# Attention and dense layer for one decoded token: early projection and half of a value unit moved into the loop, bias rows on four partitions, last value chunks of 48, 8, 8 tiles

## The chip, the cores and the metric

One core of one Trainium2 chip. Times are device microseconds (us) of an execution; a kernel is executed several times and the medians and single times are quoted. The kernel before takes 669.57 us (median of three, 669.31 to 669.69).

## The reference, cut to what matters

```python
# B=8 batch rows, one token each, D=512; 32 query heads, 8 key/value heads, 8192 cached positions, Dh=128
mod = (silu(c) @ w_mod).reshape(8, 6, 1, -1)            # six modulation vectors
h = layernorm(x) * (1 + ca) + sa
q = (h @ wq).reshape(B, 1, 32, 128)
p = softmax(q @ k_cache^T * Dh ** -0.5)                 # per batch row: 16 MiB of keys
o = p @ v_cache                                         # per batch row: 16 MiB of values
x = x + ga * (o.reshape(B, 1, 4096) @ wo)               # output projection, wo is 4 MiB
h = layernorm(x) * (1 + cb) + sb
x = x + gb * (relu(h @ w1 + b1) ** 2 @ w2 + b2)         # two dense layers, F = 1792
```

All tensors are bf16. The caches are 268 of the 284 MB that the kernel moves.

## The kernel before

Keys and values stream through a ring of four 4 MiB slots. One pass of a hardware loop works on one batch row: four key units, softmax, four value units 0 to 3. The program is recorded as a list of operations, each with its dependences; a helper then gives every engine its instruction stream, with a loop of eight passes. The output of eight heads is projected once, behind the loop (the part called "post").

The part that turned out to matter is how the helper writes the loop:

```python
def _looped(self, e, eng, passes):
    ...
    for i in range(passes):
        for p in "ab":
            for j, o in enumerate(self._part(e, (i, p))):
                want = self._want(e, o, i)
                # semaphores that are counted per pass: the wait stays with its instruction
                inside = {s: v for s, v in want.items() if s in per}
                ...
                # all others: the wait is written here, ahead of the loop
                self._emit(eng, None, {s: v for s, v in want.items() if s not in per}, seen)
    with nc.Fori(0, passes, engines=[pe], ...) as i:
        for j, o in enumerate(self._part(e, (0, "a"))):
            self._emit(eng, o, first["a", j], seen)
        ...
        with eng.If(i < passes - 1):          # part "b": not in the last pass
            for j, o in enumerate(self._part(e, (0, "b"))): ...
    for o in self._part(e, "post"):           # the tail
        self._emit(eng, o, self._want(e, o, passes - 1), after)
```

A slot of the ring is loaded again as soon as TensorE releases it, four units ahead. So each load is issued when TensorE reaches a certain place in its work. The loads at the start, in the order of the queue:

```python
load(0)
load(1)                                              # two key units of pass 1
d_b1 = dma("sync", s_bb, ... b1_row <- B_b1)
d_b2 = dma("sync", s_bb, ... b2_row <- B_b2)
d_wo = dma("sync", s_wo, ... wo_sb <- A_wo)          # 4 MiB, output projection
load(2)
load(3)
...
def project(k_oP):                                   # called once, in "post"
    for g in range(6):
        for j in range(4):
            t = op("tensor", ... e.matmul(bank(7)[32 * j:32 * (j + 1), :], oP[:, g, ...],
                    wo_sb[:, 4 * g + j, :], start=(g == 0), stop=(g == 5), ...), [k_oP, d_wo])
```

The last value unit (unit 3 of pass 8) arrives in four pieces that end at tiles 64, 96, 112 and 128 of 128, and TensorE takes them up one by one; behind them come the weights of the two dense layers.

Of the kernel before, what the change touches and what calls it, by code (L numbers as in the profile page):

```python
# [5 lines left out]
ACT = mybir.ActivationFunctionType  # L6
ALU = mybir.AluOpType
# [161 lines left out]
def bass_adaLN_cond__gqa_block_cached__dense_activation_squared_relu__decode_kernel(  # L169
# [17 lines left out]
    with ExitStack() as es:  # L187
# [29 lines left out]
        ONE8 = sb("ONE8", [1, B], BF16)  # L217
        PERM = sb("PERM", [128, 4, 32], BF16)
# [8 lines left out]
        b_row = sb("b_row", [1, F + D], BF16)  # L227
# [26 lines left out]
        oP = KF[:, 2816:3072].rearrange("p (g j b) -> p g j b", g=8, j=4)  # L254
        proj = KF[:, 4096:5120].bitcast(FP32)
        b1_row, b2_row = b_row[:, 0:F], b_row[:, F:F + D]
# [23 lines left out]
        s_last = [sem(f"d_l{i}") for i in range(4)]  # L280
# [25 lines left out]
        t = pool(lambda e: e.memset(ONE8[:], 1.0))  # L306
# [33 lines left out]
        t = select(PERM[:], [[-1, 4], [-4, 32]], 0, 1, 1.0, NE, t)  # L340
# [7 lines left out]
        CH = (64, 96, 112, 128)  # L348
        F2 = FT - 2

        def load(n):
            kv, b, p = units[n]
            s = n % NSLOT
            src = (A_k_cache if kv == "k" else A_v_cache)[b, 2 * p:2 * p + 2]
            src = src.rearrange("g s d -> (g s d)").rearrange("(p f) -> p f", p=128)
            dep = [released.get(s)]
            if units[n] == last:
                t0, toks = 0, []
                for i, t1 in enumerate(CH):
                    toks.append(dma("sync", s_last[i], lambda e, a=t0 * DH, z=t1 * DH: e.dma_start(  # L360
                        RING[:, s, a:z], src[:, a:z]), dep))
                    t0 = t1
                loaded[n] = toks
            else:
                loaded[n] = dma("sync", s_ring[s], lambda e: e.dma_start(slot(s), src), dep)
# [75 lines left out]

        k_sb = op("vector", lambda e: e.tensor_copy(hbT[:, :, 1, :], mod(3)), [k_modT])
# [6 lines left out]
        d_b1 = dma("sync", s_bb, lambda e: e.dma_start(b1_row, B_b1.rearrange("(o f) -> o f", o=1)))  # L449
        d_b2 = dma("sync", s_bb, lambda e: e.dma_start(b2_row, B_b2.rearrange("(o f) -> o f", o=1)))  # L450
# [56 lines left out]
        hT_ps = [bank(i)[:, 0:16 * 7].rearrange("p (f a b) -> p f a b", f=7, a=2) for i in range(2)]  # L507
        yT_ps = bank(2)[:, 0:KT * B].rearrange("p (k b) -> p k b", k=KT)

        def permute(q0, q1, dst, deps):  # L510
            pP = bank(6)[:, 64 * q0:64 * q1].rearrange("p (g j b) -> p g j b", j=4, b=B)
            for hl in range(REP):
                for j in range(4):
                    t = op("tensor", lambda e, hl=hl, j=j: e.matmul(
                        pP[32 * hl:32 * (hl + 1), :, j, :].rearrange("p (q h) b -> p h q b", h=2),
                        PERM[:, j, :], oTn_p[:, :, q0:q1, hl, :], start=True, stop=True,
                        tile_position=(0, 32 * hl)), deps)
            return op("vector", lambda e: e.tensor_copy(dst, pP), [t])

        def project(k_oP):  # L520
            for g in range(6):
                for j in range(4):
                    t = op("tensor", lambda e, g=g, j=j: e.matmul(
                        bank(7)[32 * j:32 * (j + 1), :], oP[:, g, :, :].rearrange("p j b -> p (j b)"),
                        wo_sb[:, 4 * g + j, :], start=(g == 0), stop=(g == 5), tile_position=(0, 32 * j)),
                        [k_oP, d_wo])
            return op("vector", lambda e: e.tensor_copy(proj, bank(7)), [t])

        for b in range(B):
# [23 lines left out]
            pe_stream(1, 4)  # L553
# [5 lines left out]
            pe_stream(1, 4)  # L559
# [32 lines left out]
            turn_acts(pe_stream(3, 1))  # L592
# [3 lines left out]
            pe_stream(2, 1)  # L596
# [9 lines left out]
            for p in range(NP):  # L606
                if p == NP - 1:
                    Pg.at = "post" if lastb else (b, "b")
# [3 lines left out]
                lastu = units[n] == last  # L612
                if not lastu:
                    for m in range(32):
                        cg = m % 4
                        t = op("tensor", lambda e, p=p, m=m, cg=cg, vt=vt, Obank=Obank: e.matmul(  # L616
                            Obank[32 * cg:32 * (cg + 1), :], lhs[:, p, 32 * m:32 * m + 32],
                            vt[:, 4 * m:4 * m + 4, :], start=(m < 4), stop=(m >= 28),
                            tile_position=(0, 32 * cg)),
                            [loaded[n], k_rinv] + pmd[m // 8])  # L620
# [3 lines left out]
                    elif p == NP - 2:  # L624
                        pe_stream(3, 4)
# [13 lines left out]
                    elif p == NP - 2:  # L639
                        pe_stream(1, 4)  # L640
# [3 lines left out]
                    if lastb and p == NP - 2:  # L644
                        Pg.at = "post"
                        k_proj = project(permute(0, 3, oP[:, 0:6], [norm_last, k_all] + stg_free + hold))
                        for k in range(KT):
                            op("tensor", lambda e, k=k: e.matmul(
                                yT_ps[:, k, :], b2_row[:, k * 128:(k + 1) * 128], ONE8[:, :],
                                start=(k == 0), stop=False, skip_group_check=True), [d_b2, s_bank_free[2]])  # L650
                else:
# [15 lines left out]
                    def direct(a, z, i):  # L667
                        for m in range(a, z):
                            t = op("tensor", lambda e, m=m: e.matmul(
                                oT_w, vt[:, m, :], wide(lhs[:, NP - 1, 8 * m:8 * m + 8]), start=False,  # L670
                                stop=(m == z - 1), skip_group_check=True), [loaded[n][i], k_rinv] + pmd[m // 32])
                        return t

                    for m in range(28):
                        cg = m % 4
                        t = op("tensor", lambda e, m=m, cg=cg, vt=vt: e.matmul(
                            bank(3)[32 * cg:32 * (cg + 1), :], lhs[:, NP - 1, 32 * m:32 * m + 32],
                            vt[:, 4 * m:4 * m + 4, :], start=(m < 4), stop=(m >= 24),
                            tile_position=(0, 32 * cg)),
                            [loaded[n][0 if m < 16 else 1 if m < 24 else 2], k_rinv] + pmd[m // 8])  # L680
                        if m == 15:
                            for f in range(FT):
                                op("tensor", lambda e, f=f: e.matmul(
                                    hT_ps[f // 7][:, f % 7, 1, :], fcol(b1_row, f), ONE8[:, :],
                                    start=(f % 7 == 0), stop=False, skip_group_check=True), [d_b2, s_bank_free[f // 7]])
                            for k in range(KT):
                                op("tensor", lambda e, k=k: e.matmul(
                                    attn_ps[:, k, :], proj[:, 128 * k:128 * (k + 1)], SELP[:, :],
                                    start=(k == 0), stop=False, skip_group_check=True), [k_proj])
                    osb = O_sb[:, 1, :]  # L690
                    t = op("vector", lambda e: e.tensor_copy(osb, bank(3)), [t])
                    for i in range(4):
                        op("tensor", lambda e, i=i: e.matmul(
                            oT_ps, osb[:, i * 128:(i + 1) * 128], SEL[:, i, :], start=(i == 0), stop=False,
                            skip_group_check=True), [t, k_all])
                    t = direct(112, 128, 3)
# [3 lines left out]
                    k_oP = permute(3, 4, oP[:, 6:8], [t])  # L700
                    for g in (6, 7):
                        for j in range(4):
                            for k in range(KT):
                                k_attn = op("tensor", lambda e, g=g, j=j, k=k: e.matmul(
                                    attn_ps[:, k, :], wo_sb[:, 4 * g + j, k * 128:(k + 1) * 128], oP[:, g, j, :],
# [9 lines left out]
        o_ps = bank(4)[:, 0:256]  # L715
        for cc in range(2):
            for k in range(2):
                op("tensor", lambda e, k=k, cc=cc: e.matmul(
                    o_ps[64 * cc:64 * cc + B, 128 * k:128 * (k + 1)], x1T[:, 2 * cc + k, :], IDENT[:, :],
                    start=(k == 0), stop=False, tile_position=(0, 64 * cc), skip_group_check=True), [k_x1])  # L720
# [9 lines left out]
        rsb = rstd2[:].unsqueeze(1).to_broadcast([128, 7, B])  # L730
        for k in range(KT):
# [4 lines left out]
            for f in range(FT):  # L736
                t = op("tensor", lambda e, f=f, k=k: e.matmul(
                    hT_ps[f // 7][:, f % 7, :, :], wcol(k, f), hbT[:, k, :, :], start=False, stop=(k == KT - 1),
                    skip_group_check=True), [k_hb, k_sb, d_w1[k // (KT - 1)]])
                if k == KT - 1 and f % 7 == 6:  # L740
                    hh = f // 7
                    fs = slice(7 * hh, 7 * (hh + 1))
                    t = op("vector", lambda e, hh=hh, fs=fs: e.tensor_tensor(
                        rT[:, fs, :], hT_ps[hh][:, :, 0, :], rsb, ALU.mult), [t, k_rstd])
# [3 lines left out]
                        hidT[:, fs, :], rT[:, fs, :], 0.0, rT[:, fs, :], ALU.max, ALU.mult), [t]))  # L748
        for f in range(FT):
            for k in range(KT):  # L750
                t = op("tensor", lambda e, f=f, k=k: e.matmul(
                    yT_ps[:, k, :], W2v[:, f, k * 128:(k + 1) * 128], hidT[:, f, :],
                    start=False, stop=(f == FT - 1), skip_group_check=True), [k_sq[f // 7], d_w2[f // 4]])
# [47 lines left out]
```

## Time and profile before

| | before |
|---|---|
| median (range) | 669.57 us (669.31 to 669.69) |
| span of the profiled execution | 667.6 us |
| TensorE busy | 513.8 us, 77% |
| a pass of the loop | 77.6 to 77.7 us, DMA share 1.00 |
| last weights landed | 664.16 us |

### The profile page before, as it was taken

To read this page: it belongs to the slowest core of one execution; us is meant where nothing else is said; L and a number is where in the kernel's file an instruction comes from. 1 tells how busy PE (TensorE), PEld (TensorE's weight loads), DVE (VectorE), ACT (ScalarE), POOL (GpSimd) and SP (SyncE) were. 2 spreads that over 40 slices of the span, in tenths; PEclk is the share of its full clock that TensorE was granted. 3 is DMA by queue.
4 is the path that set the end of the run, shared out by engine and by line. 5 is a ranking of instruction groups with operands and counts; after the bars stand their busy time and mean duration, and the time that the engine had idled before them with its cause. 6 is when DMAs were issued, how large, how long until landed. Compare 5 with 4: busy or idle time off the path is not lost.

```text
span 667.6 us, 15485 instructions
## 1 busy us (share of the span) xinstructions
PE 513.8 (77%) x7064; PEld 344.8 (52%) x7064; DVE 302.6 (45%) x571; ACT 258.7 (39%) x289; POOL 18.4 (3%) x76
## 2 busy tenths in 40 slices
PE   3493984898739985699848987499756998389885
PEld 2283731675328742577317853287425773177534
DVE  2262731566216651367314662166513673156722
ACT  2151640466105660266404662066502654046610
POOL 7300000000000000000000000000000000000000
PEclk9696997899969998699977999699987999779996
DMA  9999999999999999999999999999999999999996
GB/s 376 431 412 437 426 427 435 432 430 430 434 434 430 430 432 436 428 432 432 436 428 430 434 434 430 430 434 434 428 432 434 434 426 434 432 434 428 434 415 264
DMA packets 12176, 283.85 MB, mean 425 GB/s; under 512 B 1250, under 2 KB 1283, under 8 KB 3588
## 3 DMA queue, kind: packets, MB, share of 16 engines
q1 hardware_dynamic: 12116, 283.65, 99.1%
q8 instruction: 9, 0.15, 0.1%
q10 hardware_dynamic: 48, 0.02, 0.0%
q14 instruction: 3, 0.02, 0.0%
HBM read 283.66 MB, written 0.01 MB: 425 GB/s over the span
## 4 chain that ended last, share of the span: by engine, by line
PE 52%; DMA 37%; ACT 7%; DVE 2%; SPq 1%; issue 1%
PE PS L479 36%; DMA ring<-in_A_k_cache_dram 32%; PE PS L496 9%; ACT P_sb L562 5%; PE PS L616 2%; DMA ring<-in_B_w_dram 2%; DMA ring<-in_A_wq_dram 2%; PE PS L469 1%; SPq L659 1%; ACT KTb L484 1%; DVE O_sb L626 1%; PE PS L463 1%; PE PS L574 1%; DVE Pm L588 0%; PE PS L594 0%
## 5 line engine op out<-in xcount | busy, mean ns | idle before, releaser
L484 ACT ACTIVATE KTb<-PS 128x1024 bf16<-128x1024 bf16 x192 | 196.5, 1024 | 332.2 <-PE PS L479 332.2
L479 PE MATMUL PS<-IDENT,ring 128*128 128x128 bf16 x4096 | 267.4, 227 | 51.2 <-DMA ring<-in_A_k_cache_dram 51.2
L479 PEld LDWEIGHTS PS<-IDENT,ring 128*128 128x128 bf16 x4096 | 246.8, 102 | 99.6 <-DMA ring<-in_A_k_cache_dram 52.4
L486 DVE COPY KTb<-PS 128x1024 bf16<-128x1024 bf16 x320 | 210.1, 687 | 143.9 <-PE PS L479 141.8
L616 PE MATMUL PS<-ring,Pm 128*32 128x512 bf16 x992 | 70.4, 434 | 46.8 <-DMA ring<-in_A_v_cache_dram 45.9
L496 PE MATMUL PS<-KTb,Qb 128*32 128x512 bf16 x1024 | 78.8, 385 | 4.5 <-ACT KTb L484 4.5
L626 DVE CAST O_sb<-PS 128x512 bf16<-128x512 f32 x31 | 21.4, 692 | 126.7 <-PE PS L616 126.7
L616 PEld LDWEIGHTS PS<-ring,Pm 128*32 128x32 bf16 x992 | 26.8, 106 | 85.5 <-DMA ring<-in_A_v_cache_dram 54.4
L562 ACT ACTIVATE P_sb<-PS,negm 128x1024 bf16<-128x1024 f32 x32 | 35.2, 1112 | 20.2 <-DVE negm L557 20.2
L469 PE MATMUL PS<-ONES 128*128 128x512 f32 x80 | 42.1, 630 | 0.0
L574 PE MATMUL PS<-IDENT,P_sb 128*128 128x128 bf16 x256 | 19.9, 220 | 15.4 <-ACT P_sb L562 15.4
L588 DVE COPY Pm<-PS 64x512 bf16<-64x512 bf16 x48 | 20.2, 421 | 25.0 <-PE PS L574 24.5
L574 PEld LDWEIGHTS PS<-IDENT,P_sb 128*128 128x128 bf16 x256 | 14.4, 98 | 25.1 <-ACT P_sb L562 25.1
L463 PE MATMUL PS<-IDENT 128*128 128x512 bf16 x88 | 26.9, 380 | 0.0
L496 PEld LDWEIGHTS PS<-KTb,Qb 128*32 128x32 bf16 x1024 | 15.4, 94 | 21.1 <-ACT KTb L484 8.5
L503 DVE TENSOR_REDUCE m<-PS 128x1 f32<-128x512 f32 x32 | 22.0, 689 | 6.6 <-PE PS L496 6.6
L630 PEld LDWEIGHTS PS<-SEL,O_sb 128*128 128x128 bf16 x124 | 5.8, 97 | 30.5 <-DVE O_sb L626 30.5
L469 PEld LDWEIGHTS PS<-ONES 128*128 128x128 f32 x80 | 12.7, 190 | 10.6 <-issue 10.6
L630 PE MATMUL PS<-SEL,O_sb 128*128 128x8 bf16 x124 | 7.9, 169 | 12.4 <-DVE O_sb L626 12.0
L641 DVE TENSOR_TENSOR oTn<-PS,rinv 128x8 f32 x31 | 6.0, 194 | 14.9 <-PE PS L630 14.9
L463 PEld LDWEIGHTS PS<-IDENT 128*128 128x128 bf16 x88 | 7.7, 105 | 9.1 <-issue 7.2
L484 ACT ACT_TABLE_LOAD x8 | 10.3, 1283 | 3.2 <-issue 3.2
(132 smaller groups left out, 115.9 us busy)
## 6 DMA issues: line engine op xcount, KB each, us to landing
ring<-in_A_k_cache_dram SPq DMA_DIRECT2D x32, 4096.0 KB, 34.2
ring<-in_A_v_cache_dram SPq DMA_DIRECT2D x31, 4096.0 KB, 27.8
ring<-in_A_wq_dram SPq DMA_DIRECT2D x1, 4096.0 KB, 19.9
wo_sb<-in_A_wo_dram SPq DMA_DIRECT2D x1, 4096.0 KB, 47.6
ring<-in_w_mod_dram SPq DMA_DIRECT2D x1, 3072.0 KB, 10.3
ring<-in_A_v_cache_dram SPq DMA_DIRECT2D x1, 2048.0 KB, 22.6
ring<-in_B_w_dram SPq DMA_DIRECT2D x3, 512.0 KB, 19.4
ring<-in_B_w_dram SPq DMA_DIRECT2D x1, 1344.0 KB, 17.9
```

Source lines behind the costliest of these rows:

```text
L463: ts = [op("tensor", lambda e: e.matmul(bank(at).rearrange("p (a r) -> p a r", a=4), IDENT[:, :], rhs)) for _ in range(n)]
L469: ts = [op("tensor", lambda e: e.matmul(bank(at).rearrange("p (a r) -> p a r", a=4), ONES[:, :], rhs)) for _ in range(n)]
L479: t = op("tensor", lambda e, j=j, i=i: e.matmul(STG[j][:, i, :], src[:, 32 * k + 8 * j + i, :], IDENT[:, :], is_transpose=True), [loaded[n ...
L484: stg_free[j] = op("scalar", lambda e, j=j, dst=dst: e.activation(dst, STG[j], ACT.Copy), [t])
L486: stg_free[j] = op("vector", lambda e, j=j, dst=dst: e.tensor_copy(dst, STG[j]), [t])
L496: t = op("tensor", lambda e, hf=hf, q=q, rhs=rhs: e.matmul(PS[32 * q:32 * (q + 1), k, :], Qb[:, 2 * p + hf, :], rhs, start=(p == 0 and hf ...
L503: return op("vector", lambda e: e.tensor_reduce(m4[:, k:k + 1], bank(k), AX.X, ALU.max), [t])
L562: exps.append(op("scalar", lambda e, k=k: e.activation(P_sb[:, k, :, :, :], bank(k).rearrange("p (i x) -> p i x", i=8).unsqueeze(2).to_bro ...
L574: t = op("tensor", lambda e, k=k, i=i: e.matmul(STG[k][:, i, :], P_sb[:, k, i, :, :].rearrange("p h x -> p (h x)"), IDENT[:, :], is_transp ...
L588: done.append(op("vector", lambda e, dst=dst, frm=frm: e.tensor_copy(dst, frm), [t, k_pm]))
L616: t = op("tensor", lambda e, p=p, m=m, cg=cg, vt=vt, Obank=Obank: e.matmul(Obank[32 * cg:32 * (cg + 1), :], lhs[:, p, 32 * m:32 * m + 32], ...
L626: t = op("vector", lambda e, osb=osb, Obank=Obank: e.tensor_copy(osb, Obank), [t])
```

## The change

Intent: shorten what stands between the last bytes and the end. The projection of the first three value units goes ahead of unit 3, and with it the first half of unit 3, into the part of the loop that every pass executes, so that the tail starts later in the work. The biases lie on four partitions, so that 18 small matmuls become 11. The last value unit is cut so that only 8 + 8 tiles remain for the end, and four identity matmuls move between the weights of the last layer. Core of the diff (index changes, new memsets and the rearranged bias loads are cut):

```diff
-        CH = (64, 96, 112, 128)
+        CH = (64, 112, 120, 128)
...
+        def permute_early(deps):              # 4 matmuls, 1 filler, 4 copies (2 VectorE, 2 ScalarE)
...
         def project(k_oP):
             for g in range(6):
                 for j in range(4):
...
-                        [k_oP, d_wo])
-            return op("vector", lambda e: e.tensor_copy(proj, bank(7)), [t])
+                        k_oP + [d_wo])
+            return t
...
             for p in range(NP):
-                if p == NP - 1:
-                    Pg.at = "post" if lastb else (b, "b")
...
+                if p == NP - 1:
+                    proj_done = project(permute_early([norm_last, k_all] + stg_free + hold))
+                    values(0, 16, 28)
+                    Pg.at = "post" if lastb else (b, "b")
                 if not lastu:
-                    for m in range(32): ...
+                    t = values(0 if p < NP - 1 else 16, 32, 28)
...
-                    if lastb and p == NP - 2:
-                        Pg.at = "post"
-                        k_proj = project(permute(0, 3, oP[:, 0:6], ...))
-                        for k in range(KT):                       # 4 bias matmuls
...
-                    for m in range(28): ...                       # 14 bias matmuls after m == 15
+                    k_proj = op("vector", lambda e: e.tensor_copy(proj, bank(7)), [proj_done])
+                    ...                                           # 11 bias matmuls
+                    partial(range(0, 4))
+                    t = values(16, 28, 24)
...
-                    t = direct(112, 128, 3)
+                    direct(CH[1], CH[2], 2)
...
+                    t = direct(CH[2], CH[3], 3)
...                                            # five filler matmuls per pass taken out
-        o_ps = bank(4)[:, 0:256]               # 4 identity matmuls, before the first dense layer
+            if f == 8: ...                     # now inside the second dense layer
```

## The prediction

> **What bounds the kernel now.** I read the page first (engine shares, DMA line), then the windows of single passes, then the chain of waits and the timeline of the last 30 us, then the DMA view of that stretch.
>
> The program is eight passes of a loop (one batch row each: four key units, softmax, four value units 0 to 3, each unit 4 MiB) and then a tail: end of the last value unit, output projection, layer norm, two small dense layers. Page and windows of three passes of the loop:
>
> ```profile
> DMA packets 12176, 283.85 MB, mean 425 GB/s; under 512 B 1250, under 2 KB 1283, under 8 KB 3588
> 175.10:252.80 77.70, 61.23 (x841) 40.93 (x840) 36.09 (x67) 31.53 (x35) 0.00 (x0) 0.91 1.00 431
> 252.80:330.40 77.60, 61.52 (x836) 41.35 (x840) 36.47 (x66) 31.53 (x35) 0.00 (x0) 0.89 1.00 432
> 330.40:408.10 77.70, 61.92 (x836) 41.64 (x832) 36.59 (x66) 31.52 (x35) 0.00 (x0) 0.89 1.00 432
> ```
>
> The last two numbers of a window are DMA share and GB/s. The share is 1.00 in each pass, at 431 to 432 GB/s, and TensorE is busy 61 of 77.7 us: the loop is the time of its bytes (33.55 MB / 432 GB/s = 77.7 us). Nothing done by an engine there counts, unless it frees a buffer so late that the queue runs dry.
>
> The tail, in the timeline:
>
> ```profile
> 646.42 0.69 DVE L626 CAST O_sb<-PS 128x512 bf16<-128x512 f32 x1 [3.38 <-PE PS L616]
> 648.64 1.48 PE L523 MATMUL PS<-wo_sb,KTb 128*32 128x512 bf16 x24 [0.51 <-DVE KTb L518]
> 650.23 1.05 PE L676 MATMUL PS<-ring,Pm 128*32 128x512 bf16 x16
> 651.74 1.06 PE L687 MATMUL PS<-SELP,KTb 128*128 128x8 f32 x8
> 652.73 0.83 PE L676 MATMUL PS<-ring,Pm 128*32 128x512 bf16 x12
> 653.61 0.69 DVE L691 CAST O_sb<-PS 128x512 bf16<-128x512 f32 x1 [2.75 <-PE PS L676]
> 655.07 0.19 DVE L697 TENSOR_TENSOR oTn<-PS,rinv 128x8 bf16<-128x8 f32 x1 [0.76 <-PE PS L669]
> 658.30 1.53 PE L737 MATMUL PS<-hbT,ring 128*128 128x16 bf16 x42 [0.20 <-DVE hbT L724]
> 661.68 1.02 PE L751 MATMUL PS<-KTb,ring 128*128 128x8 bf16 x32 [0.98 <-DVE KTb L747]
> 663.57 1.01 PE L751 MATMUL PS<-KTb,ring 128*128 128x8 bf16 x24 [0.87 <-DMA ring<-in_B_w_dram]
> ```
>
> The chain of waits from 634 us on ends so:
>
> ```profile
> 649.42 14.74 DMA ring<-in_B_w_dram
> 664.16 0.05 issue
> 664.21 0.39 PE PS L751 x8
> 664.60 0.02 issue
> 664.62 0.20 DVE KTb L754
> ```
>
> So even here the landing of the second dense layer's weights (third piece 663.52, fourth 664.16) sets the end; 3.4 us of fixed work follow to 667.6. The compute path comes second: its first 32 matmuls of that layer end at 662.70, 0.87 us before the third piece lets it go on. What is worth gaining is thus about 0.9 to 1.5 us, and only if the landing moves.
>
> Why do the last bytes land so late? In two windows, DMA share and rate are again the last two numbers; then the DMA view of 651 to 664 us:
>
> ```profile
> 660.00:662.00 2.00, 1.02 (x28) 0.93 (x28) 1.19 (x6) 0.27 (x1) 0.00 (x0) 0.50 0.80 308
> 662.00:664.00 2.00, 1.13 (x43) 1.04 (x39) 0.22 (x1) 0.00 (x0) 0.00 (x0) 0.50 0.12 42
> q8 instruction: 2, 0.03, 1.0%
> ```
>
> A share of 0.12 is two of 16 DMA engines: stragglers. In the packet records every engine but one is done by 662.70; the last 2 KB packets of one end at 663.74. The two packets of the instruction queue are 16 KiB each, at 652.52 (1.07 us) and 661.23 (1.10 us). Before the first, no engine leads the late group at the last value piece (all done 653.74); after it a single one is late by 0.1 us (660.89 against 660.78 at the second weight piece), after the second it is 1.0 us late. I read this as one engine that carries both instruction packets.
>
> [...]the page lists nine such packets, seven during pass 1 (31.8 to 102.9 us), none in passes 2 to 8, two in the tail; and a pass has 834 matmuls, with its weight loads 1668 instructions[...]. [...]the granted clock here is 0.50 from 656 us to the end, but 128x8 matmuls still take 32 ns each (1.02 us / 32)[...].
>
> **The change part by part.**
>
> 1. Early projection in every pass. Removed per pass: five 128x512 filler matmuls (about 0.27 us each, 0.81 us for 3), 1.35 us. Added: 4 permuting matmuls (about 0.3 us by the old 16), one filler inside it, four copies of 32x192 (two VectorE, two ScalarE, about 0.36 us each by the old 128x192 cast), 24 projection matmuls at 1.48 us. They run between value units 2 and 3, where in a pass TensorE is idle from 569.84 to 576.35 us (6.5 us) waiting for unit 3. The added 2.5 us fit, and each pass keeps its 77.7 us: 0.
>
> 2. The same in the last pass. There unit 3 follows closely. Old: norm of unit 2 at 647.76, cast done 648.59, projection over 650.12. New: two copies in sequence on VectorE instead of one, 0.36 us later, so projection over about 650.6; first 16 value matmuls to 651.6.
>
> 3. Biases: 18 small matmuls (0.25 + 0.60 us) become 11, about 0.4 us. The projection's fp32 partial sums keep 1.06 us: done at 651.6 + 0.4 + 1.0 = 653.1.
>
> 4. Pieces of 64, 48, 8, 8 tiles instead of 64, 32, 16, 16. Bytes and packets are the same (4 x 128), so the fourth still lands at 654.23, and the second now where the third did, 652.97. All 12 value matmuls begin only then, behind step 3: 653.1 + 0.85 = 653.95, 0.4 us later than the old 653.56. Cast to 654.7, selection 654.75, last 8 direct matmuls instead of 16 (0.28 instead of 0.55): norm at about 655.25 against 655.07. Net +0.2 us on the compute path.
>
> 5. Four identity matmuls (0.38 us) move from before the first dense layer, where TensorE waited for VectorE anyway, to between the first 32 and the last 24 matmuls of the second. Compute path: 662.70 + 0.2 = 662.9, plus 0.3 is 663.2 before the last 24, then 24 x 32 ns = 0.77: 663.95, against 664.60 in the old. Possible gain 0.65 us, if the weights are there.
>
> 6. Instructions after the loop fall from 283 matmuls to 220, and the loop grows from 834 to 857[...]. [...]With one fetch, the late engine ends at 660.89 + 1.27 + 0.65 = 662.81. If the second packet comes after it, the fourth piece lands near 663.2 and step 5's 0.65 us come through; if just before its last packets, the landing stays at 664.1 and the gain is zero. I call it even, with a slight lean to the gain: 0.55 x 0.65 = 0.36 us.
>
> 7. Start: more memsets, and wider selects on POOL, about 1 us before the loop; the first key unit lands at 30.7 us, POOL ended at 26.85. Hidden.
>
> Sum: 669.57 - 0.4, rounded with room for the landing's own scatter: **669.1 us**.
>
> **Rivals.** (a) The landing does not move: DMA-bound to the last packet, time 669.5. For it: the chain above is DMA, and no byte is removed. (b) Second fetch harmless and the compute path not delayed by step 4: 668.5. For it: the last fetch is at the edge. (c) The later value matmuls, or a jump out of the loop in the middle of unit 3, cost more than 0.3 us and the compute path takes over: 670 or more. Against it: the old exit was hidden in a wait of 0.46 us for VectorE. (d) Fewer fillers let the clock fall in the softmax, or loop code no longer fits: every pass would suffer, but a value unit at half clock (3.6 instead of 1.9 us) still hides under DMA, with 14.7 us of loads queued when a key load is issued (561.6 to the landing of unit 3 at 576.35).
>
> **Range and chances.** Between (b) less 0.5 and (c) plus 0.3: 668.0 to 670.3. Two per cent is 13.4 us; only an unhidden 1.7 us in every pass would give that. Faster 0.01, same 0.98, slower 0.01.
>
> **What would show it.** Passes still 77.6 to 77.7 us at share 1.00; unit 3 of a pass still ended by its DMA; last value matmuls from about 653.1; norm of unit 3 near 655.25; instruction packets near 655.8 and 662.5 to 663; last weight landing near 663.2 (gain) or 664.1 (none). I am wrong if the passes change, if instruction packets appear in passes 2 to 8, or if TensorE waits at the loop's exit.

0.55 x 0.65 us is 0.36 us, and 669.57 - 0.4 came, rounded, to the 669.1 us that stand there. The "nine such packets" are the 16 KiB packets of the page's line "q8 instruction". Rival (d) can be read with what the trace of the kernel before has: in the wait of 6.5 us in front of unit 3 of pass 7 the granted clock went from 1.00 (571 to 573 us) to 0.50 (574 to 580), and the unit's matmuls took 3.60 us, against 1.91 for those of unit 2. And the waits for the last weights there ended with the last of sixteen shares: fifteen of the fourth piece had landed by 663.14 us, the last at 664.16, and the eight matmuls behind it began at 664.21.

## More of the kernel before

The prediction shows the windows, the tail and the chain of waits. What it does not show is the start. First the waits of TensorE in the kernel before: in a line stand the waiting group, what it waited for, then us in total, times and longest wait.

```profile
PE PS L479 <- DMA ring<-in_A_k_cache_dram: 51.2, 9, 10.1
PE PS L616 <- DMA ring<-in_A_v_cache_dram: 45.9, 10, 6.5
```

And the queue engine SP's timeline of its load issues (start, and time to the end of the group's last issue):

```profile
3.68 0.40 SPq L451 DMA_DIRECT2D wo_sb<-in_A_wo_dram  x1
14.59 23.87 SPq L365 DMA_DIRECT2D ring<-in_A_k_cache_dram  x2
41.47 41.43 SPq L365 DMA_DIRECT2D ring<-in_A_v_cache_dram  x4
95.68 8.03 SPq L365 DMA_DIRECT2D ring<-in_A_k_cache_dram  x3
```

TensorE waits for keys and values, and for nothing else longer than 4.5 us at a time. The value loads of pass 1 begin at 41.47 us and the key loads of pass 2 at 95.68, while the value unit in front of them lands at 110.00: the queue has 14 us of work in hand. The output weights, issued at 3.68 us, wait in no line: they are used only behind the loop.

## The result, and the profile after

| | before | after |
|---|---|---|
| executions, us | 669.57, 669.31, 669.69, 669.28 | 668.67 (profiled), 670.67, 671.37, 670.54 |
| median | 669.44 (four executions) | 670.61 |
| ratio after / before | | 1.0013, 95% interval 0.9991 to 1.0034: same |
| span of the profiled execution | 667.6 | 666.6 |
| last weights landed in it | 664.16 | 662.98 |

A ratio here is the mean time of one kernel's executions over that of the other's of the same rounds, so it is not quite the ratio of the medians. The "same" came as predicted, the number did not: 670.61 lies 0.3 us above the predicted range and 1.5 us above the predicted time. And the profiled execution, the only one of the four with a trace, is the one that took 668.67 us.

Its passes are as predicted. Two windows of one pass each (length, then busy time of PE, PEld, DVE, ACT, POOL, then clock, DMA share, GB/s), and the page's line of the instruction queue:

```profile
174.60:252.20 77.60, 65.80 (x931) 43.54 (x931) 38.09 (x70) 32.19 (x37) 0.00 (x0) 0.93 1.00 432
252.20:329.80 77.60, 61.69 (x863) 41.55 (x862) 37.20 (x68) 32.19 (x37) 0.00 (x0) 0.93 1.00 432
q8 instruction: 9, 0.15, 0.1%
```

Share 1.00 at 432 GB/s; nine instruction packets, seven of them in pass 1. So is its tail, in the timeline:

```profile
652.82 0.83 PE L641 MATMUL PS<-ring,Pm 128*32 128x512 bf16 x12
654.95 0.19 DVE L723 TENSOR_TENSOR oTn<-PS,rinv 128x8 bf16<-128x8 f32 x1 [0.56 <-PE PS L693]
661.60 1.01 PE L778 MATMUL PS<-KTb,ring 128*128 128x8 bf16 x32 [1.00 <-DVE KTb L767]
662.54 0.38 PE L774 MATMUL PS<-IDENT,x1T 128*8 128x128 bf16 x4
662.86 0.80 PE L778 MATMUL PS<-KTb,ring 128*128 128x8 bf16 x24
```

The last 24 matmuls are no longer preceded by a wait for the weights (before: 0.87 us), and no DMA stands near the end of the chain of waits any more:

```profile
661.60 1.01 PE PS L778 x32
662.61 0.31 PE PS L774 x4
662.92 0.75 PE PS L778 x24
663.70 0.20 DVE KTb L781
```

What nobody had asked about is the start. Waits of TensorE in the changed kernel:

```profile
PE PS L488 <- DMA ring<-in_A_k_cache_dram: 33.3, 6, 6.7
PE PS L488 <- DMA wo_sb<-in_A_wo_dram: 25.5, 1, 25.5
PE PS L641 <- DMA ring<-in_A_v_cache_dram: 15.2, 7, 3.3
```

The beginning of its chain of waits, and SP's load issues:

```profile
4.13 46.77 DMA wo_sb<-in_A_wo_dram
50.90 0.70 issue
51.60 6.58 PE PS L488 x64
```

```profile
15.20 23.43 SPq L369 DMA_DIRECT2D ring<-in_A_k_cache_dram  x2
63.40 29.59 SPq L369 DMA_DIRECT2D ring<-in_A_v_cache_dram  x4
105.79 3.31 SPq L369 DMA_DIRECT2D ring<-in_A_k_cache_dram  x2
```

L488 is the transposing of keys. It does not use the output weights, and yet it waits 25.5 us for them, once: TensorE's first pass begins at 51.6 us, where the first key unit had landed at about 31. The projection now stands inside the loop; the semaphore of the output weights is not counted per pass; so the helper writes its wait ahead of the loop, ahead of everything that the loop does. With TensorE 21 us late, the value loads of pass 1 are issued at 63.40 us instead of 41.47, and the first key load of pass 2 at 105.79 instead of 95.68. The value unit in front of that key load lands at 109.88. Of the 14 us in hand, 4 are left, and since DMA engines finish their shares of a unit at different times (the sixteen shares of that value unit landed between 107.93 and 109.88 us) and an idle engine's first packet of a load comes 1.0 to 1.5 us after the issue (read in late_one's trace, below; in the kernel before, the first load was issued at 0.81 us and its first packet came at 1.84), the margin is small.

### The profile page after: what moved, and what is told of

It is laid out like the page before. It is cut to its first block, busy times and chain, and to the rows that moved or that the text cites. A ratio compares the mean times of both kernels' runs of the same rounds, so it can differ in the third digit from the quotient of the medians.

```text
span 666.6 us, 15803 instructions
## 1 busy us (share of the span) xinstructions
PE 518.3 (78%) x7201; PEld 350.3 (53%) x7201; DVE 308.0 (46%) x586; ACT 264.0 (40%) x305; POOL 20.4 (3%) x79
## 4 chain that ended last, share of the span: by engine, by line
PE 55%; DMA 32%; ACT 6%; DVE 4%; issue 1%; POOL 0%; ACTq 0%; SPq 0%; DVEq 0%; POOLq 0%
PE PS L488 38%; DMA ring<-in_A_k_cache_dram 21%; PE PS L505 10%; DMA wo_sb<-in_A_wo_dram 7%; ACT P_sb L587 5%; DMA ring<-in_A_v_cache_dram 4%; PE PS L641 3%; ACT KTb L493 1%; DVE O_sb L659 1%; DVE m L512 1%; PE PS L599 1%; PE PS L550 1%; PE PS L619 0%; DVE Pm L613 0%; PE PS L478 0%
## 5 line engine op out<-in xcount | busy, mean ns | idle before, releaser
L488 PE MATMUL PS<-IDENT,ring 128*128 128x128 bf16 x4096 | 267.8, 228 | 60.7 <-DMA ring<-in_A_k_cache_dram 33.3
L488 PEld LDWEIGHTS PS<-IDENT,ring 128*128 128x128 bf16 x4096 | 247.3, 102 | 108.9 <-issue 49.4
L641 PE MATMUL PS<-ring,Pm 128*32 128x512 bf16 x1020 | 66.9, 407 | 17.9 <-DMA ring<-in_A_v_cache_dram 15.2
L542 ACT ACTIVATE KTb<-PS 32x192 bf16<-32x192 f32 x16 | 5.2, 322 | 103.6 <-PE PS L472 103.4
L550 PE MATMUL PS<-wo_sb,KTb 128*32 128x512 bf16 x192 | 15.4, 467 | 6.8 <-ACT KTb L542 6.8
L472 PE MATMUL PS<-IDENT 128*128 128x512 bf16 x48 | 15.7, 381 | 0.0
L550 PEld LDWEIGHTS PS<-wo_sb,KTb 128*32 128x32 bf16 x192 | 5.9, 108 | 14.0 <-DVE KTb L544 9.5
```

The source lines that it names most:

```text
L488: t = op("tensor", lambda e, j=j, i=i: e.matmul(STG[j][:, i, :], src[:, 32 * k + 8 * j + i, :], IDENT[:, :], is_transpose=True), [loaded[n ...
L550: t = op("tensor", lambda e, g=g, j=j: e.matmul(bank(7)[32 * j:32 * (j + 1), :], oPe[:, 3 * (g % 2) + g // 2, :, :].rearrange("p j b -> p ...
L641: t = op("tensor", lambda e, m=m, cg=cg, p=p, vt=vt, Obank=Obank: e.matmul(Obank[32 * cg:32 * (cg + 1), :], lhs[:, p, 32 * m:32 * m + 32], ...
```

## The experiments

Three theories. **S** (start): the wait ahead of the loop leaves the key load of pass 2 so late that in some executions the DMA engines run dry; what is lost there is lost for good, because from then on the queue is always full (DMA share 1.00 in the two windows above). **E** (end): nothing is wrong with the start; in some executions an instruction packet (16 KiB, 1.1 us of one DMA engine) meets the engine that still carries the last weights, as the prediction feared in its step 6. **R** (rest): the four first executions were a matter of chance. (A fourth, **C** in the expectation of after_again, blames the first chip; it was not tested. The record names the chips of the later runs, 11, 6, 4, 15 and 3, and not that of the first session.) A key to read them all is one table, taken from the traces; its columns are explained here once. "Issued" is when the first key load of pass 2 is issued. "Interval" is how long after the unit before it that unit landed; 9.71 us is a unit at full rate, more is time lost. "Last weights" is the landing of the fourth piece of the second dense layer's weights, counted from the landing of value unit 2 of pass 8, so free of what happened earlier.

| profiled kernel | time of that execution | issued | interval | last weights |
|---|---|---|---|---|
| before | 669.43 | 95.68 | 9.72 | 19.86 |
| before_wait | 669.42 | 104.32 | 9.72 | 19.48 |
| after | 668.67 | 105.79 | 9.75 | 18.84 |
| after_again | 669.65 | 104.94 | 9.71 | 18.86 |
| after_third | 668.89 | 105.33 | 9.71 | 18.88 |
| after_fourth | 668.99 | 104.40 | 9.72 | 18.86 |
| after_fifth | 668.92 | 103.96 | 9.71 | 18.88 |
| wait_in_loop | 668.72 | 95.69 | 9.71 | 18.86 |
| wait_in_loop_2 | 669.25 | 96.99 | 9.71 | 18.87 |
| wait_in_loop_3 | 669.14 | 95.92 | 9.71 | 18.88 |
| after_slot40 | 669.73 | 105.46 | 9.70 | 20.05 |
| late_half | 669.44 | 107.03 | 10.39 | 18.95 |
| late_one | 671.08 | 108.83 | 12.04 | 19.18 |
| late_two | 675.07 | 111.19 | 11.73 | 20.45 |
| in_loop_late_two | 668.69 | 94.04 | 9.72 | 18.88 |
| after_loop | 668.89 | 96.59 | 9.71 | 18.87 |
| pad_tail | 669.66 | 98.44 | 9.70 | 18.86 |
| pad_loop_20 | 669.46 | 96.61 | 9.71 | 20.07 |

(The kernel before was profiled in an execution of its own, 669.43 us, which is not among the four of the table above. Value unit 0 of pass 1 also has a longer interval where TensorE starts late: 10.05 to 10.49 us in the changed kernel and in before_wait, 12.38 in late_two, against 9.71. Up to 10.5 us nothing remains of it at the next units: the second key unit of pass 2 landed at 129.31 us in the first profile of the changed kernel and at 129.37 in that of wait_in_loop. In late_two it does cost: 2.67 us there, 2.02 at the key unit and 1.59 at the last weights come to 6.3 us, against 6.2 between its median and that of after_third.)

### The changed kernel again

after_again, after_third, after_fourth and after_fifth are the changed kernel without an edit, each beside other runs on another chip or at another time.

> The changed kernel unchanged, to see the spread of its times. Its first profile agreed with the prediction's better branch (668.67 us), but three timed executions took 670.5 to 671.4 us. Theory S (start): the projection inside the loop moved TensorE's wait for the output weights ahead of the loop (25.5 us before pass 1), which leaves the load queue only 4 to 7.6 us of queued work in pass 1; in some executions it runs dry. Then times scatter over 668.5 to 671.5 us, before stays at 669.3 to 669.7. Theory E (end): the second instruction fetch meets the last weights in some executions and not in others; then times fall in two groups about 1.1 us apart, near 668.7 and 669.8, and none is over 670.3. Theory C (chip): the first chip was to blame; then all lie near 668.7.

Measured: 669.65, 669.54, 668.90, 668.99, 669.23 us; median 669.23, ratio 0.9992 (0.9979 to 1.0006).

> The changed kernel once more, beside the dosed ones. Theory S in its sharper form: ahead of pass 2 the load of its first key unit is issued at about 105.8 us, when the queue holds work to 109.9 us (to 107.4 us on the fastest DMA engine)[...], so the changed kernel runs with no margin. Then 668.6 to 671.5 us, and in the profile the issue of that load lies between 104.5 and 109 us; where it is over 107.5 the landing of that unit is later than the landing before it plus 9.75 us. Theory R (only the chance by which instruction packets delay the slowest DMA engine): 668.6 to 670 us, no relation to that issue.

Measured: 668.89, 668.72, 669.03, 669.48, 668.95; median 668.95, ratio 0.9991 (0.9978 to 1.0005).

> The changed kernel once more, on another chip. Theory S (the wait for the output weights ahead of the loop leaves the key load for pass 2 with about no time in hand): 668.6 to 671.5 us, executions scattered by chip and moment; in the profile the first key load of pass 2 is issued between 104.8 and 106.5 us. If the issue is below 105.5 the unit lands 9.7 us after the one before it. Rival R (a last-weights collision at the end alone makes the slow executions): the same scatter as in the kernel with the wait inside the loop.

Measured: 668.99, 670.63, 668.80, 668.77, 668.68; median 668.80, ratio 0.9995 (0.9981 to 1.0008).

> The changed kernel beside them: 668.6 to 671.4 us. If the profile catches an execution above 670: E has the fourth piece 19.5 us or more after the second last value unit and the key unit of pass 2 at 9.71 us after the one before; S has the fourth piece at 18.86 and the key unit 10 us or more after the one before.

Measured: 668.92, 669.26, 669.10, 669.04, 668.71; median 669.04, ratio 0.9991 (0.9978 to 1.0005).

With the first four, the changed kernel has 24 executions: median 669.01 us, four of them above 670 (670.54, 670.63, 670.67, 671.37). The kernel before has 41: median 669.50, three above 670 (670.16, 670.30, 670.54). So the typical time of the changed kernel is half a microsecond below the one before and 0.1 us from the prediction, though no single session's interval excludes a ratio of 1; the first median was made of three slow executions out of four. The slow ones are not spread evenly: three of the first four, one of the later twenty. If they fell at random among the 24, three or four would land in the first four in less than 1% of all orders (81 of 10626), so chance alone, R, is a weak explanation, and something particular to that session (the chip, C, or the moment) stays untested. Two things the record does settle. The extra time lies inside the kernel: the spans of the four are 668.6 to 669.3 us, those of the other 20 at most 667.6. And the granted TensorE clock does not set them apart: it was 0.946, 0.916, 0.946 and 0.914 in the four, 0.912 to 0.945 in the others. None of the five profiles caught one of the slow ones.

### The wait moved into the loop

wait_in_loop is the changed kernel; its wait for the output weights stands with the first projection matmul.

```diff
-                        k_oP + [d_wo])
+                    def one(e, g=g, j=j):
+                        if g == 0 and j == 0:
+                            e.wait_ge(s_wo, 16)
+                        return e.matmul(...)
+                    t = op("tensor", one, k_oP)
```

> The changed kernel, only that TensorE waits for the output weights at the first projection matmul inside the loop instead of ahead of it (the semaphore keeps its value, so passes 2 to 8 go through). Theory S: TensorE starts pass 1 near 30.9 us instead of 51.6, the load of the first value unit is issued near 41.5 instead of 63.4 us, and the slow executions vanish: 668.4 to 669.0 us, scatter under 0.5 us. Theory E: the same scatter as the changed kernel in the same rounds, within 0.3 us of its mean.

Measured: 668.72, 669.14, 668.87, 668.92, 669.56; median 668.92, ratio 0.9992 (0.9978 to 1.0005). SP's issues are those of the kernel before again:

```profile
41.62 41.28 SPq L369 DMA_DIRECT2D ring<-in_A_v_cache_dram  x4
95.69 8.03 SPq L369 DMA_DIRECT2D ring<-in_A_k_cache_dram  x3
```

So the late start comes from where that wait is written and from nothing else. The time gained by its repair is too small for these runs to show, and the scatter, 0.84 us, is over the 0.5 that S asked for. (The run was correct, so passes 2 to 8 went through the wait.) The same kernel twice more:

> The changed kernel with the wait for the output weights inside the loop, on the same chip. S: 668.6 to 669.4 us, no execution above 670 unless the kernel before has such executions too, TensorE starts at 31 us, the key load for pass 2 is issued at 95.7. R: as the changed kernel of the same rounds.

Measured: 669.25, 668.92, 669.26, 668.71, 670.02; median 669.25, ratio 0.9995 (0.9981 to 1.0008); in the same rounds the changed kernel had 0.9995 as well.

> The base of the two on the same chip: 668.6 to 669.3 us as a rule, at most one execution in five above 670.

Measured: 669.14, 671.05, 668.85, 668.83, 669.22; median 669.14, ratio 0.9998 (0.9985 to 1.0012). Two of its 15 executions lie above 670, one at 671.05, although S cannot act here: the key load of pass 2 has 14 us in hand. S alone therefore does not explain slow executions of this size.

### The wait alone, in the kernel before

```diff
+        Pg.wait("tensor", [d_wo])        # ahead of the loop
         load(2)
```

> The kernel before with one wait added: TensorE waits for the output weights ahead of the loop, as the changed kernel does. Nothing else differs. Theory S: it becomes slower and scattered, about +1 us in the mean over the kernel before (670 to 671.5 us in most executions). Theory E: no change, 669.2 to 669.9 us, because the loads still queue in time.

Measured: 669.42, 670.09, 670.64, 670.14, 669.52; median 670.09, ratio 1.0006 (0.9992 to 1.0020). The loads move as in the changed kernel (key load at 104.32), and the profiled execution has lost nothing at that unit (9.72 us). The time is unclear between "nothing" and +0.6 us; by the spans, which leave out what lies around the kernel, it is +0.2 (median 667.8 against 667.6 in the same rounds). S had expected most executions at 670 to 671.5 us, and three of five lie above 670.

### A dose of lateness

If S is a real mechanism, a TensorE that starts still later must lose time at exactly that unit. POOL memsets between the landing of the output weights and TensorE's first matmul provide the delay: about 1.75, 3.5 and 7 us (POOL is busy 23.9 us in late_one, 20.4 in the changed kernel).

```diff
+        late = [d_wo]
+        for _ in range(1):               # late_two: range(2); late_half: one of half the size
+            late = [pool(lambda e: e.memset(P_sb[...], 0.0), late)]
+        Pg.wait("tensor", late)
```

> The changed kernel with one 3.5 us memset on POOL between the landing of the output weights and TensorE's start of pass 1, so TensorE starts 3.5 us later still. Theory S: the load for pass 2 is issued near 109.3 us[...]: 1 to 2 us over the changed kernel's best, 669.8 to 671.2 us. Theory R: within 0.4 us of the changed kernel in these rounds.

Measured: 671.08, 671.02, 670.42, 671.41; median 671.05, ratio 1.0020 (1.0004 to 1.0035).

> The same with two such memsets, TensorE 7 us later. Theory S: the first value load of pass 1 is issued near 70.4 us and the load for pass 2 near 112.8, 4 to 6 us are lost for good: 673 to 675 us. Theory R: within 0.4 us of the changed kernel.

Measured: 675.07, 675.15, 679.22, 673.37; median 675.11, ratio 1.0094 (1.0061 to 1.0127).

> One memset of half the size (about 1.75 us) between the landing of the output weights and TensorE's first matmul: half of the dose that gave 671.05 us. S: the key load for pass 2 is issued near 107, its unit lands 9.9 to 10.8 us after the one before it, and the time is 669.3 to 670.6, between the changed kernel and the full dose. R, or a loss that comes from something else of the full dose: as the changed kernel, within 0.3 us.

Measured: 669.44, 669.59, 669.48, 669.47, 671.80; median 669.48, ratio 1.0008 (0.9994 to 1.0021).

The windows 105 to 110 and 110 to 115 us, first of the changed kernel, then of late_half, then of late_one (the last two numbers are DMA share and GB/s):

```profile
105.00:110.00 5.00, 4.42 (x45) 2.07 (x46) 1.60 (x4) 0.00 (x0) 0.00 (x0) 1.00 1.00 419
110.00:115.00 5.00, 3.98 (x45) 1.40 (x43) 1.39 (x4) 0.32 (x1) 0.00 (x0) 1.00 1.02 436
```

```profile
105.00:110.00 5.00, 4.20 (x63) 1.84 (x55) 1.58 (x3) 0.00 (x0) 0.00 (x0) 1.00 0.96 374
110.00:115.00 5.00, 4.51 (x45) 1.61 (x42) 0.97 (x3) 0.00 (x0) 0.00 (x0) 1.00 1.02 436
```

```profile
105.00:110.00 5.00, 3.88 (x63) 1.97 (x67) 1.25 (x3) 0.00 (x0) 0.00 (x0) 1.00 0.88 334
110.00:115.00 5.00, 5.00 (x54) 1.99 (x48) 0.89 (x2) 0.00 (x0) 0.00 (x0) 1.00 0.85 347
```

The hole grows with the dose: the unit lands 0.68 us late after 1.75 us of delay and 2.33 us late after 3.5 us, and the medians follow: 669.48 is 0.68 us above the changed kernel's 668.80 of the same rounds, 671.05 is 2.10 above 668.95. (The intervals of the ratios overlap for the two smaller doses; only late_two stands clear of the changed kernel by time alone.) Between the issue times, loss begins at about 107.03 - 0.68 = 106.4 us (an estimate: past the edge, a microsecond later is a microsecond lost; late_one gives 108.83 - 2.33 = 106.5). The changed kernel issues between 103.96 and 105.79 in its five profiles. Its margin is 0.6 to 2.4 us, where the kernel before had 11. Counted from the landing of the unit in front (110.0 to 110.1 us), the load lost time here when it was issued less than about 3.5 us ahead. In the profile with the least margin, after itself, a trace of it may be seen (9.75 us, 0.04 over a full-rate unit).

The control has the two memsets of late_two, but released by the first key unit, with the wait for the output weights inside the loop:

> The control: the version whose wait is inside the loop, with the same two memsets between the landing of the first key unit and TensorE's start (start near 38 us instead of 30.9). Theory S: 7 us fit into the 14 us of margin that this version has, 668.5 to 669.3 us. If a delay of TensorE alone costs time whatever the queue holds, it is slower by several us.

Measured: 668.69, 670.40, 670.42, 668.64; median 669.55, ratio 1.0003 (0.9988 to 1.0018). The interval is 9.72 us: the 5.6 us between the medians of late_two and of this control do not come from the memsets, they come from where the memsets stand. But two of four executions are slow, by 1.7 us, and again S is not at hand.

### Only the tail

after_loop keeps everything but the place of the early projection and of the first half of unit 3, which stay behind the loop; then no wait is written ahead of it.

```diff
                 if p == NP - 1:
-                    proj_done = project(permute_early(...))
-                    values(0, 16, 28)
                     Pg.at = "post" if lastb else (b, "b")
+                    if lastb:
+                        proj_done = project(permute_early(...))
+                        values(0, 16, 28)
...
-                    t = values(0 if p < NP - 1 else 16, 32, 28)
+                    t = values(0, 32, 28)
```

> The changed kernel with the early projection and the first half of unit 3 only behind the loop, as in the kernel before; biases on four rows and the pieces of 48, 8, 8 kept. There is no wait ahead of the loop then. S: TensorE starts at 31 us, the key load for pass 2 is issued at 95.7, 668.5 to 669.4 us, as the kernel with the wait in the loop: the gain in the tail does not need the projection in the common part. Rival: the projection of pass 8 between the last value matmuls costs time at the end, then 669.3 to 669.8, as before.

Measured: 668.89, 669.84, 670.87, 669.80, 669.62; median 669.80, ratio 1.0007 (0.9993 to 1.0020); the changed kernel had 668.80 in the same rounds. The profiled execution is as good as any (668.89, weights at 18.87), the other four are not. On these five executions the projection inside the loop looks better by a microsecond; the intervals of the two ratios overlap, though, and with only the good execution profiled no cause is seen.

### The instruction packets at the end

after_slot40 shifts the loop's start by 40 instructions, to make the instruction packets of the tail come earlier.

```diff
-        with nc.Fori(..., head_slot={pe: 0} ...) as i:
+        with nc.Fori(..., head_slot={pe: 40} ...) as i:
```

> The changed kernel with the loop's first TensorE instruction 40 slots further into its 16 KiB block[...]: the two packets near 653.5 to 654.5 and 660.5 to 661.8 us instead of 655.07 and 662.24. Theory E: the second packet now always meets the last weights, their landing moves from 662.98 to about 664 us, and the time is 0.7 to 1.1 us above the fast executions of the changed kernel. Theory S: the same scatter as the changed kernel; the tail of the profile shows the later landing all the same, if the fetch goes to the engine that is already late.

Measured: 669.73, 669.67, 668.88, 669.65, 670.01; median 669.67, ratio 0.9998 (0.9984 to 1.0012). The first packet of the tail came at 654.36 us instead of 655.07, the second at 662.28 as before: the expected shift of the second was a miss. Yet the fourth piece landed 20.05 us after value unit 2, 1.2 us later than in the changed kernel. The median is 0.4 us above the changed kernel's of the same rounds (669.23), less than the 0.7 to 1.1 that E had asked for.

pad_tail puts 60 small matmuls into TensorE's idle stretches of the tail of wait_in_loop; pad_loop puts the same 60 into each pass, where TensorE waits for unit 2. (Matmuls of this shape, 128x8, took 32 ns each in the tail of the kernel before: 1.02 us / 32.)

```diff
+        def small(n):
+            for _ in range(n):
+                op("tensor", lambda e: e.matmul(bank(...)[:, 0:8], IDENT[:, :], IDENT[:, 0:8]))
# pad_tail: small(14), small(8), small(10), small(14), small(14) at five places behind the loop
# pad_loop: small(60) after value unit 1; pad_loop_20: small(20); pad_loop_34: small(34)
```

> Wait inside the loop, plus 60 small matmuls (128x8, an estimated 0.03 us each) spread over five idle stretches of TensorE in the tail. The second instruction packet of the tail moves from 662.1 to 662.3 us to between 659.5 and 661.5, ahead of the last weights' packets. Theory E: the packet costs its engine 1.1 us while that engine still has weights to fetch, so the fourth piece lands 19.5 to 20.1 us after the second last value unit instead of 18.86, in the profile and in most executions: 669.5 to 670.5 us. Rival: instruction packets at the end don't matter, then 668.7 to 669.3 as the base.

Measured: 669.66, 669.45, 669.52, 671.04, 669.66; median 669.66, ratio 1.0005 (0.9991 to 1.0018). The expectation failed: the second packet stayed at 662.25 us and the weights at 18.86. The half microsecond comes from elsewhere. The groups of the two dense layers start at 659.12 and 662.53 us; in the base, at 658.62 and 662.02. In gaps of 0.3 to 0.5 us, on the chain that ended last, these small matmuls were not free: the first group started 0.50 us later, the second 0.51. As a test of E it says nothing.

> Wait inside the loop, plus the same 60 small matmuls in each pass, after the second value unit, where TensorE waits for its DMA. The loop has 917 matmuls, 1834 instructions with their weight loads[...]: no packets in passes 2 to 8. [...]E: one packet instead of two, fourth piece 18.86 after the second last value unit unless it meets the slowest engine, 668.6 to 669.3 us and less scatter than the base. Rival: the filler work costs time in each pass or evicts loop code, then 670 or more.

Measured: 682.52, 682.99, 681.93, 684.28, 681.72; median 682.52, ratio 1.0196 (1.0182 to 1.0210). The DMA view of one pass, 174.6 to 252.2 us, first of the changed kernel, then of pad_loop:

```profile
DMA packets 1150, 33.49 MB, mean 432 GB/s; under 512 B 128, under 2 KB 128, under 8 KB 128
q1 hardware_dynamic: 1150, 33.49, 100.3%
```

```profile
DMA packets 1149, 33.31 MB, mean 429 GB/s; under 512 B 128, under 2 KB 128, under 8 KB 128
q1 hardware_dynamic: 1140, 33.16, 99.6%
q8 instruction: 9, 0.15, 0.8%
```

Code of the loop is fetched again: nine packets in this pass, 73 in all instead of 9. The profiled execution takes 13.4 us more than the base (682.52 against 669.14). Of these, 12.2 us had been lost when value unit 2 of pass 8 landed (656.62 against 644.38), with 62 extra packets up to there, 0.20 us each; the rest came in the tail.

The counts in the expectations are of operations in the program. The trace has six more matmuls in a pass, because each of the six fp32 operations stands in it as two (ten records for five fillers, two for the sum): 863 in the changed kernel, 923 in pad_loop, 883 in pad_loop_20, 897 in pad_loop_34. With a weight load each (the page of the changed kernel counts 7201 of both) that is 1726, 1846, 1766 and 1794 instructions, without the loop's own control. Where the edge lies was to be seen from two counts in between. ("No packets" stands for an edge above the count, "packets in each pass" for one below.)

> Wait inside the loop, 20 small matmuls more in each pass: 877 matmuls, 1754 instructions with their weight loads. [...]no instruction packets in passes 2 to 8, two in the tail, 668.6 to 671 us as the base. If the edge lies right above the changed kernel's 1714: packets in each pass and 675 us or more, and refetching becomes a suspect for the slow executions.

Measured (one execution): 669.46 us, before beside it 669.43. Nine packets, none in passes 2 to 8: the code of 883 matmuls was not fetched again. By luck this profile caught the late landing that E is about. In its timeline the last eight matmuls wait for the fourth piece, as those of after_slot40 do:

```profile
662.95 0.59 PE L786 MATMUL PS<-KTb,ring 128*128 128x8 bf16 x16
664.27 0.38 PE L786 MATMUL PS<-KTb,ring 128*128 128x8 bf16 x8 [0.73 <-DMA ring<-in_B_w_dram]
```

and its chain of waits ends in the DMA, like that of the kernel before:

```profile
649.96 14.26 DMA ring<-in_B_w_dram
664.27 0.39 PE PS L786 x8
```

In both traces fifteen of the sixteen DMA engines have finished the fourth piece by 663.03 us (after_slot40: 663.21), and the last comes 1.2 us later, at 664.23 (664.41). One engine is late by about the length of a packet, and the second packet began at 662.10 (662.28) and took 1.10 us: that fits E, though the records do not name the engine. In the first profile of the changed kernel the packet ran from 662.24 to 663.34, past the last completion at 662.98, so its engine had no weights left to carry.

> 34 small matmuls more in each pass: 891 matmuls, 1782 instructions[...]. [...]packets in each pass and about 680 us; [...]none, 668.6 to 671 us.

Measured (one execution): 678.45 us. The page:

```profile
q8 instruction: 45, 0.74, 0.5%
```

Seven are of pass 1 and two of the tail; the other 36 come in four rounds of nine, which begin at 269, 426, 512 and 591 us, as passes 4, 6, 7 and 8 start. Passes 2, 3 and 5 have none. So code was fetched again in four of seven passes with 1794 instructions, and in none with 1766, in one execution each. The changed kernel, with 1726, stands 40 below a count without refetching and 68 below one with it; its five profiles show no packet in passes 2 to 8.

## Why the prediction was right or wrong

**The passes (step 1): their length was right, "they fit" was incomplete.** 77.60 us at share 1.00, as stated, and the fillers are not missed (granted clock 0.93 in both windows, 0.89 to 0.91 in those of the kernel before). But the step looked only at TensorE's idle time inside a pass. Moving the projection into the loop also moved its dependence on the output weights, and the helper that writes the loop puts such a wait ahead of it. That took 21 us from TensorE's start and all but 0.6 to 2.4 us of the queue's margin. Step 7, "hidden", missed it too: at the start it counted POOL's instructions and no wait that the loop sends ahead; TensorE's first pass began at 51.6 us, not near 31. wait_in_loop shows the cause, the three doses show the mechanism. In the five profiles of the changed kernel it cost next to nothing: 0.04 us at most by the landings, and by the bytes carried between 105 and 129 us 0.16 us at most (10.29 MB in the first profile, 10.36 in wait_in_loop). The list of what would prove the prediction wrong named waits at the loop's exit, and none at its entrance.

**The last pass, biases, pieces (steps 2 to 4): right, a little pessimistic.** Last 12 value matmuls from 652.82 (predicted 653.1), norm of unit 3 at 654.95 (655.25).

**Identity matmuls and the compute path (step 5): right.** Its last 24 matmuls ended at 663.66 in the first profile, 663.95 predicted.

**Instruction packets and the landing (step 6): right in kind, luckier than "even".** Packets came at 655.07 and 662.24, predicted near 655.8 and 662.5 to 663. The last weights landed at 18.84 to 18.88 us after value unit 2 in all five profiles of the changed kernel, against 19.86 in the kernel before: a microsecond earlier, so that the compute path sets the end. The other outcome exists as well: 20.05 and 20.07 in after_slot40 and pad_loop_20, with 0.74 and 0.73 us of wait. What sets the time of a packet was not shown. The working, now cut, had it move with every matmul added in front; yet 60 added in the tail left the second packet at 662.25 (pad_tail), and 20 more in each pass at 662.10 (pad_loop_20), while with a later or an older tail it came at 663.43 (late_one), 667.53 (late_two) and 661.23 (before). Its counts were off, too: a pass has 840 matmuls in the trace before and 863 after, not 834 and 857, and the difference is 23, not 24.

**The sum was right, the range was not.** 669.1 was predicted; 24 executions have the median 669.01, against 669.50 before (41 executions). That closeness is partly luck: 669.1 averages two outcomes of step 6, and all five profiles show the better one, which alone would have been 668.9 (669.57 - 0.65). The step that failed is the range: its upper end, "(c) plus 0.3", 670.3, stood for a cost in the tail that did not arise, and its scatter was that of three executions of the kernel before, which lie within 0.4 us. The prediction has no term for an execution that is slower as a whole. The runs showed one: four of 24 lie 1.5 to 2.4 us above the changed kernel's median. Three of the first four did, and the median fell outside.

**What those slow executions are stays open.** S has the right size: a TensorE 3 us later gives 670.42 to 671.41, the very times of the first session. But the profiles show an issue at 105.79 at the latest, and it would take 108.8. And kernels where S cannot act have them too: six of 29 executions of wait_in_loop, in_loop_late_two, after_loop and pad_tail lie above 670, up to 671.05. E is seen in profiles, but those executions took 669.46 and 669.73 us, against 668.67 to 669.65 where the weights came early, and not 671. Refetched loop code would have the size (1.7 us a pass in pad_loop, 12.2 over seven passes) and has shown itself in no profile of a kernel of up to 883 matmuls in the loop. What set the first session apart, C included, was not tested. None of the profiles is of a slow execution of the changed kernel, so no cause is claimed.

**A better version?** wait_in_loop has the gain of the tail and the full margin at the start. Its 15 executions have the median 669.14, within what separates the four later sessions of the changed kernel (668.80 to 669.23), so it is safer by its margin and not shown to be faster.

## What to carry to other kernels

When work moves into a loop, its dependences move too: look where the generated code puts each wait, and ask of every load what its issue waits for and how much work the queue still holds at that moment. A margin can be used up without any change of the time; only a dose of extra delay shows how much is left. And take the range of a prediction from the scatter of many executions: with a gain of half a microsecond, four are not enough for a median.
